# Three sets of steps in a hand-ordered FFT, MLP and mixture kernel: the middle x tile, the first S load and one load of the inverse's input

## The chip, the cores and the metric

One Trainium2 chip, one of its cores. The metric is the device time of one execution in microseconds (us), the median of several. TensorE is called PE here, VectorE DVE, ScalarE ACT, GpSimd POOL; SP is the engine whose queue issues nearly all DMAs.

## What is computed

For each of 8 batches of 3072 tokens by 256 channels: a long filter by way of the Fourier transform, then over all 24576 tokens a squared-ReLU MLP, then a soft mixture of 8 experts with 32 slots.

```python
X = np.fft.rfft(x, axis=1); y = np.fft.irfft(X * (filt_r + 1j * filt_i), n=3072, axis=1)
t = y.reshape(8 * 3072, 256)
h = np.maximum(t @ w_in, 0.0); t = h * h @ w_out
logits = t @ phi
d = softmax over tokens(logits);  slot_in = d.T @ t
slot_out[e] = np.maximum(slot_in[e] @ w1[e], 0.0) @ w2[e]
out = softmax over slots(logits) @ slot_out
```

All data is float32; the wide layer runs as three matmuls on parts of float32r, "high" and "low".

## The kernel before, in words

The tokens go through the MLP in 48 chunks of 512, six to a batch. A chunk is 8 *pairs* of the loop over `P`; a pair takes 2 steps of a common clock, so a chunk is 16 steps. In a pair, `layer` (L594, L595, L596) computes 2 x 128 features: high weights by high `xo`, high weights by low `xo`, low weights by high `xo`. `square` squares the ReLU, the odd half on POOL (L605), `turn_h` transposes it on DVE (L622), `move` sends it by DMA to a buffer `hd` in another layout (L651), and `logit` (L663) takes its product with the folded weights, in blocks of 16 matmuls every four pairs. `slot_in` (L794) multiplies `hd` of the previous chunk with the exponentials.

Between these pieces stands all other work, written into five streams (`dsp`, `mv`, `late`, `fft`, `w`) as events with a step number. `run_streams(t)` lets each stream go on in the order of its steps as far as step `t`; within one step the streams run in the order named. There is no other scheduler: the instructions stand on each engine in the order in which these functions write them, and a DMA stands on SP's queue where its function stood.

The transform of batch b runs while the batch before it goes through the MLP; its steps (`when`, `LEAD`, in the block at L1136 to L1158) count from the start of that earlier batch, so a negative step lies in the batch before that. One transform of batches 3 to 7, in its order:

- three x tiles of 1 MB (s = 0, 1, 2), each by four DMAs of 256 KB (`load_x`, L143); each is folded in two halves k = 0, 1 (`fold_x`): the sum on DVE (L155) into a small tile, the difference on POOL in place (L156). Then 16 matmuls (`mm_a`, L165), four ACT copies (L172), and two stores of 512 KB to a DRAM tensor S (`store_a`, L181).
- four blocks j: S is read back in another layout by four DMAs of 192 KB (`load_s2`, L206), 64 matmuls (`mm_b`, L299), filter products (L310, L319), 64 matmuls of the inverse (`mm_g2`, L218), copies, and four stores of 192 KB to a DRAM tensor G (`store_g2`, L240).
- for each of the batch's six chunks, `load_g` (L460) reads 512 KB of G into a tile `gin`. The matmuls `mm_y` (L514), the copy L522 and the two sums L531 on DVE make rows of y from it; `lead_y` (L539, ACT) writes the high part of `xo` in two halves, `rest_y` (L546, POOL) the low part in two halves. The first `layer` of the chunk needs all four.

The chunks with `6 * b + g` 0, 1 and 6 have a plain form instead: `mm_ai` (L478), `lead_ai`, `rest_ai`. The tiles of x, S, filter and output of the transform share three buffers of 1 MB (tag `f8`).

```python
for s, (TL, TF, T) in enumerate(TA):
    put(TL, load_x, s)
    for k in range(2):
        put(TF + k, fold_x, s, k)
...
    put(T - LS[j], load_s2, j)
```

Of the kernel before, what the change touches and what calls it, by code (L numbers as in the profile page):

```python
# [38 lines left out]
def body(tc, x, cA, cAf, fwp, fwd, ivp, inv, flt, cst, w_in, w_out, phi, w1, w2, out):  # L39
# [43 lines left out]
    def put0(t, fn, *a):  # L83
        ev0[round(t, 3)].append((fn, a))
# [369 lines left out]
    def out_events(b, st, late):  # L454
# [93 lines left out]
        for g in range(NCB):  # L548
            if 6 * b + g not in (0, 1, 6):
                T = 96 * b + 16 * g - 6.5  # L550
                late(max(T - 19.5, 13.5), load_g, g)
                late(T, mm_y, g)
                late(T + 0.5, even_y, g)
                late(T + 1, unfold, g, ALU.add)
                late(T + 1, unfold, g, ALU.subtract)
                for k in range(2):
                    late(T + 2 + 2 * k, lead_y, g, k)
                    late(T + 2.5 + 2 * k, rest_y, g, k)
                continue
            T = 96 * b + 16 * g - 4  # L560
            put = late
            if T < 0:
                def put(t, fn, *a):
                    put0(ST["G0"] + ST["Gd"] * (t + 7), fn, *a)
            put(T - (5 if (b, g) == (0, 1) else 3), load_g, g)
            if T < 0:
                put(T - 1, warm)
            for k in range(2):
                put(T + k, mm_ai, g, k)
                put(T + k + 0.5, lead_ai, g, k)  # L570
                put(T + k + 0.5, rest_ai, g, k)
# [463 lines left out]
    def stream(nm, o=0):  # L1035
        def put(t, fn, *a):
            streams[nm].append((t + o, fn, a))
        return put
# [66 lines left out]
    with tc.manual_schedule():  # L1105
        put, late = stream("fft"), stream("late")
        st = {}
        put0(43.3, load_const)
        fft_events(0, lambda: first, put0, 0, 0, 0, None, st)
        out_events(0, st, late)  # L1110
        def wput(t, *a):

# [18 lines left out]
        for n in range(4):  # L1131
# [4 lines left out]
        LEAD = [  # L1136
            [[6.5, 6.5, 9.5, 9.5], [10, 7.5, 8, 10], [5, 6, 6.5, 6.5], [5.5, 10.5, 10, 10]],
            [[5.5, 7.5, 15.25, 15.25], [6.5, 12.5, 13.5, 13.5], [5, 5.5, 10, 10], [5.5, 13, 15.25, 15.25]],
            [[20.25] + [15.25] * 3, [13.5] * 4, [20.5, 10, 10, 10], [6, 15.25, 15.25, 15.25]],
        ]  # L1140

        opened = False
# [6 lines left out]
        for b in range(1, NB):  # L1149
            st = {}  # L1150
            if b == 1:
                when = ([(22, 24.5, 26.5), (24, 29, 33.5), (27.5, 32, 36.5)], [47, 54.5, 65.5, 76.5], [53, 61.5, 70.5, 81.5])
            elif b == 2:
                when = ([(-19, -15.5, -10), (-11, -7, -3), (-5.5, -3, 0)], [13.5, 22, 38, 54], [18.5, 33.5, 49.5, 65.5])
            else:
                when = ([(-41, -31, -26), (-23, -19, -14.5), (-22.5, -15.5, -10)], [1.5, 22, 38, 54], [17.5, 33.5, 49.5, 65.5])
            fft_events(b, lambda: G["fft"], stream("fft", 96 * (b - 1)), *when, dict(f=3, u=8, c=2, lead=LEAD[min(b, 3) - 1]), st)
            out_events(b, st, late)  # L1158
        for c in range(NCH - 1):
# [241 lines left out]
        for g in range(NG):  # L1401
            b, o = divmod(g, N2 // 4)
# [171 lines left out]
```

## Time and profile before

| | |
|---|---|
| median of 3 runs | 1855.48 us (1854.55 to 1858.27) |
| the profiled execution | 1859.09 us, its span 1857.3 us |
| busy, share of the span | PE 98%, DVE 65%, ACT 56%, POOL 42% |
| granted clock of TensorE, mean | 0.996 of full speed |
| DMA queue of SP | 421 MB, 78.7% of the 16 engines' span |

The span is divided by the chunks: with two blocks of a transform in it, a chunk takes some 35.4 us, without any 31.45. PE is all but always busy, so the place to look is the few waits on PE, and who ends them. A line of the timeline is: start, duration, engine, line of the code, operation, tile written <- tiles read, shape, count, and in brackets the engine's idle time before it and who ended it. SPq is SP's queue; the duration there is the time that SP spends on issuing, with the waits inside a merged row.

### The profile page before, as it was taken

Reading aid. Unit: us, or ns where it says so; the run is one execution under the profiler, and the core shown is the slowest. Engines: PE = TensorE matmul, PEld = TensorE weight load, DVE = VectorE, ACT = ScalarE, POOL = GpSimd, SP = SyncE. Lnnn points to the kernel's source line nnn. Section 1 sums busy time; section 2 is a strip of 40 time slices with the busy share of each in tenths; the row PEclk is TensorE's granted clock in tenths of the full one; section 3 lists DMA queues with packets and bytes.
Section 4 is the critical chain, followed back from the end, with each engine's and each line's share of the span. In section 5 each row is a group of like instructions: output and inputs, shape, how many; then the busy total and the mean of one; then the engine's idle time right before and its main releaser. Section 6 shows DMA issues by size and latency. Waiting matters only on the chain.

```text
span 1857.3 us, 42036 instructions
## 1 busy us (share of the span) xinstructions
PE 1812.1 (98%) x16326; PEld 1192.9 (64%) x16326; DVE 1212.9 (65%) x2267; ACT 1033.4 (56%) x1930; POOL 776.3 (42%) x812
## 2 busy tenths in 40 slices
PE   9899999999999999999999999999999999999987
PEld 6666666666666666666666666666566666666555
DVE  7856666676666666666667666666666756565558
ACT  6755555556555564555655555556555555555445
POOL 4043543454444534544444444354344443333224
PEclk9999999999999999999999999999999999999999
DMA  8669989878777896888778787687878666675999
GB/s 309 205 184 281 257 234 269 247 212 238 230 213 203 227 273 165 224 243 214 234 220 222 209 253 220 189 229 217 247 199 240 200 169 182 171 206 153 247 338 383
DMA packets 245813, 425.02 MB, mean 229 GB/s; under 512 B 25712, under 2 KB 103664, under 8 KB 245616
## 3 DMA queue, kind: packets, MB, share of 16 engines
q1 hardware_dynamic: 244744, 421.13, 78.7%
q8 instruction: 130, 2.13, 0.5%
q10 hardware_dynamic: 728, 1.15, 0.2%
q14 instruction: 67, 0.55, 0.1%
q0 software_dynamic: 144, 0.07, 0.0%
HBM read 151.71 MB, written 77.59 MB: 123 GB/s over the span
## 4 chain that ended last, share of the span: by engine, by line
PE 84%; DMA 5%; DVE 3%; SPq 2%; issue 2%; ACT 1%; POOL 1%; POOLq 0%; DVEq 0%; ACTq 0%
PE p L594 18%; PE p L595 17%; PE p L596 17%; PE L L663 9%; PE sd L794 8%; PE sd L218 3%; PE sd L299 3%; PE sd L514 2%; PE sd L165 2%; DMA f<-S 2%; SPq L651 1%; DMA hd<-hT 1%; DVE ct L1208 1%; PE pt L1197 1%; PE pt L1410 1%
## 5 line engine op out<-in xcount | busy, mean ns | idle before, releaser
L605 POOL TENSOR_TENSOR h<-h 128x512 f32<-128x512 f32 x375 | 395.1, 1054 | 837.0 <-ACT h L601 747.5
L601 ACT ACTIVATE h<-p 128x512 f32<-128x512 f32 x768 | 459.0, 598 | 348.9 <-PE p L596 334.5
L622 DVE STREAM_TRANSPOSE hT<-h 128x512 f32<-128x512 f32 x736 | 485.3, 692 | 250.4 <-ACT h L603 230.4
L594 PE MATMUL p<-xo,wiH 128*128 128x512 f32 x1534 | 621.7, 405 | 0.1
L595 PE MATMUL p<-xo,wiH 128*128 128x512 f32 x1534 | 605.6, 395 | 7.2 <-POOL xo L546 7.2
L596 PE MATMUL p<-xo,wiL 128*128 128x512 f32 x1534 | 605.8, 395 | 0.0
L594 PEld LDWEIGHTS p<-xo,wiH 128*128 128x128 f32 x1534 | 288.1, 188 | 122.4 <-issue 43.9
L595 PEld LDWEIGHTS p<-xo,wiH 128*128 128x128 f32 x1534 | 288.6, 188 | 70.0 <-POOL xo L546 9.4
L596 PEld LDWEIGHTS p<-xo,wiL 128*128 128x128 f32 x1534 | 288.3, 188 | 68.4
L603 ACT ACTIVATE h<-h 128x512 f32<-128x512 f32 x393 | 248.4, 632 | 12.5
L319 POOL TENSOR_TENSOR u<-u 128x256 f32<-128x256 f32 x224 | 160.5, 739 | 114.9 <-DVE u L310 114.9
L663 PE MATMUL L<-h,wf 128*32 128x512 f32 x1536 | 186.9, 599 | 2.2 <-DVE wf L1021 1.8
L531 DVE TENSOR_TENSOR gin<-gin,sd 128x512 f32<-128x512 f32 x90 | 61.8, 687 | 182.7 <-ACT gin L522 181.2
L522 ACT ACTIVATE gin<-sd 128x512 f32<-128x512 f32 x45 | 26.9, 598 | 256.7 <-PE sd L514 256.7
L794 PE MATMUL sd<-hd,eT 128*32 128x512 f32 x1472 | 166.3, 592 | 0.0
L310 DVE TENSOR_TENSOR u<-sd,f 128x512 f32<-128x512 f32 x240 | 152.7, 675 | 11.5 <-PE sd L299 10.1
L546 POOL TENSOR_TENSOR xo<-gin,xo 128x512 fp32r<-128x512 f32 x90 | 119.3, 1325 | 0.0
L794 PEld LDWEIGHTS sd<-hd,eT 128*32 128x32 f32 x1472 | 47.8, 110 | 110.1 <-issue 106.8
L228 ACT ACTIVATE f<-sd 128x512 f32<-128x512 f32 x112 | 61.1, 610 | 79.8 <-PE sd L218 79.8
L713 DVE TENSOR_TENSOR lo<-L,lp 128x512 fp32r<-128x512 f32 x47 | 32.3, 688 | 107.4 <-ACT lp L712 107.4
L663 PEld LDWEIGHTS L<-h,wf 128*32 128x32 f32 x1536 | 40.0, 109 | 96.2 <-issue 91.4
L770 DVE STREAM_TRANSPOSE eT<-et 32x128 f32<-32x128 f32 x184 | 72.0, 391 | 1.9
(161 smaller groups left out, 1596.2 us busy)
## 6 DMA issues: line engine op xcount, KB each, us to landing
hd<-hT SPq DMA_DIRECT2D x736, 256.0 KB
f<-flt SPq DMA_DIRECT2D x28, 1024.0 KB
gin<-G SPq DMA_DIRECT2D x47, 512.0 KB
out<-w1t SPq DMA_DIRECT2D x47, 512.0 KB
f<-x SPq DMA_DIRECT2D x84, 256.0 KB
S<-f SPq DMA_DIRECT2D x42, 512.0 KB
f<-S SPq DMA_DIRECT2D x112, 192.0 KB
G<-f SPq DMA_DIRECT2D x112, 192.0 KB
```

The costliest lines, as they stand in the source:

```text
L310: vec.tensor_tensor(out=u, in0=p.rearrange("p (h d) -> p h d", d=D), in1=f[:, 2 * r + k:2 * r + k + 1, :].to_broadcast([128, 2, D]), op=AL ...
L319: gps.tensor_tensor(out=a[:, h, :], in0=a[:, h, :], in1=b[:, 1 - h, :], op=ALU.add if h else ALU.subtract)
L546: gps.tensor_tensor(out=lo, in0=st["gi", g][:, k::2, :], in1=hi, op=ALU.subtract)
L594: pe.matmul(p, wh, x[:, 0, kk, :], start=(kk == 0), stop=False)
L595: pe.matmul(p, wh, x[:, 1, kk, :], start=False, stop=False)
L596: pe.matmul(p, wl, x[:, 0, kk, :], start=False, stop=(kk == 1))
L601: act.activation(out=h, in_=p, func=ACTF.Relu, scale=2.0 ** -8)
L603: act.activation(out=h, in_=h, func=ACTF.Square)
L605: gps.tensor_tensor(out=h, in0=h, in1=h, op=ALU.mult)
L622: vec.transpose(hT[c, f // 8][:, f // 4 % 2, :, o:o + 128], h2[P, k].rearrange("p (b t) -> p b t", b=4))
L663: pe.matmul(lg[c][32 * n:32 * n + 32, :], wf[:, f, :], h2.pop((P + n // 2, n % 2)), start=(f < 4), stop=(f >= FT - 4), tile_position=(0, 3 ...
L794: pe.matmul(S[32 * n:32 * n + 32, :], e[:, 32 * t:32 * t + 32], v, start=(t == 0), stop=(t == 3), tile_position=(0, 32 * n),)
```

## The change

Three numbers, or sets of numbers, in the order. `when` for batches 3 to 7, tile s = 1: load at -28 instead of -23, folds from -22.5 instead of -19; its matmuls stay at -14.5. `LEAD` for the same batches, last list, first entry: the S load of block 0 stands 8 steps ahead of its matmuls instead of 6. And `load_g` in the plain form: 3 steps ahead for the one chunk whose step is negative, else 5; this alters chunk 6 (batch 1, g = 0) alone, from 3 to 5.

```diff
-            put(T - (5 if (b, g) == (0, 1) else 3), load_g, g)
+            put(T - (3 if T < 0 else 5), load_g, g)
...
-            [[20.25] + [15.25] * 3, [13.5] * 4, [20.5, 10, 10, 10], [6, 15.25, 15.25, 15.25]],
+            [[20.25] + [15.25] * 3, [13.5] * 4, [20.5, 10, 10, 10], [8, 15.25, 15.25, 15.25]],
...
-                when = ([(-41, -31, -26), (-23, -19, -14.5), (-22.5, -15.5, -10)], [1.5, 22, 38, 54], [17.5, 33.5, 49.5, 65.5])
+                when = ([(-41, -31, -26), (-28, -22.5, -14.5), (-22.5, -15.5, -10)], [1.5, 22, 38, 54], [17.5, 33.5, 49.5, 65.5])
```

The order of PE and that of ACT are the same before and after, buffer numbers aside. On the other engines three places differ. The first is SP's queue around the load of the middle x tile of batch 3 (`f_5468` before, `f_5370` after; `f_5033` is the tile s = 0, `f_5479` or `f_5482` the tile s = 2, `f_5330` the last output tile of batch 2). Before:

```order
L881 DMA c_dr<-co 128x128
L240 DMA G<-f_5330 48x4x256 x4
L460 DMA gin<-G 128x1024
L181 DMA S<-f_5033 128x1024 x2
L143 DMA f_5468<-x 64x2x512 x4
L143 DMA f_5479<-x 64x2x512 x4
L651 DMA hd<-hT 128x1x512 x8
```

And now:

```order
L881 DMA c_dr<-co 128x128
L143 DMA f_5370<-x 64x2x512 x4
L240 DMA G<-f_5330 48x4x256 x4
L460 DMA gin<-G 128x1024
L181 DMA S<-f_5033 128x1024 x2
L143 DMA f_5482<-x 64x2x512 x4
L651 DMA hd<-hT 128x1x512 x8
```

The four x loads passed the four stores to G, the load of `gin` and two stores to S.

The second place is SP's queue a chunk later, where S of the same batch is complete and its first block is read (`f_5954` before, `f_5855` after). Before:

```order
L181 DMA S<-f_5468 128x1024 x2
L460 DMA gin<-G 128x1024
L181 DMA S<-f_5479 128x1024 x2
L651 DMA hd<-hT 128x1x512 x8
L206 DMA f_5954<-S 48x4x256 x4
L651 DMA hd<-hT 128x1x512 x8
```

And now:

```order
L181 DMA S<-f_5370 128x1024 x2
L460 DMA gin<-G 128x1024
L181 DMA S<-f_5482 128x1024 x2
L206 DMA f_5855<-S 48x4x256 x4
L651 DMA hd<-hT 128x1x512 x16
```

The S loads passed eight moves of h. (In batch 1 the one load of `gin` passed the two S stores of a tile in the same way, so that two loads of `gin` stand together.)

The third is POOL around the two low parts of `xo` of the first chunk after the fold, with the folds of the middle x tile. Before:

```order
L605 TENSOR_TENSOR h<-h 128x512 x5
L546 TENSOR_TENSOR xo<-gin,xo 128x512
L156 TENSOR_TENSOR f_5468<-f_5468 128x512
L605 TENSOR_TENSOR h<-h 128x512
L546 TENSOR_TENSOR xo<-gin,xo 128x512
L156 TENSOR_TENSOR f_5468<-f_5468 128x512
L605 TENSOR_TENSOR h<-h 128x512
L156 TENSOR_TENSOR f_5479<-f_5479 128x512 x2
```

And now:

```order
L605 TENSOR_TENSOR h<-h 128x512 x3
L156 TENSOR_TENSOR f_5370<-f_5370 128x512
L605 TENSOR_TENSOR h<-h 128x512
L156 TENSOR_TENSOR f_5370<-f_5370 128x512
L605 TENSOR_TENSOR h<-h 128x512
L546 TENSOR_TENSOR xo<-gin,xo 128x512
L605 TENSOR_TENSOR h<-h 128x512
L546 TENSOR_TENSOR xo<-gin,xo 128x512
L605 TENSOR_TENSOR h<-h 128x512
L156 TENSOR_TENSOR f_5482<-f_5482 128x512 x2
```

Both folds of the tile passed the first `xo` write. On DVE the two sums L155 of this tile moved with them: the first from behind L781 to the place ahead of the last transpose before L531, the second to the place right behind the two L531, ahead of L855.

## Rows read from the trace of the kernel before

**Rows 1.** Waits of PE, 427 to 1391 us: total us, times, longest.

```profile
PE p L595 <- POOL xo L546: 7.2, 5, 1.4
PE sd L299 <- DMA f<-S: 4.1, 9, 1.0
```

**Rows 2.** Timeline of PE where chunk 17 begins.

```profile
676.46 0.40 PE L596 MATMUL p<-xo,wiL 128*128 128x512 f32 x1
676.70 0.40 PE L594 MATMUL p<-xo,wiH 128*128 128x512 f32 x1
678.54 0.50 PE L595 MATMUL p<-xo,wiH 128*128 128x512 f32 x1 [1.44 <-POOL xo L546]
```

**Rows 3.** Timeline of POOL around the start of chunk 17.

```profile
671.54 1.04 POOL L605 TENSOR_TENSOR h<-h 128x512 f32<-128x512 f32 x1 [8.60 <-ACT h L601]
...
674.52 1.30 POOL L156 TENSOR_TENSOR f<-f 128x512 f32<-128x512 f32 x1 [0.63 <-DMA hd<-hT]
675.77 1.49 POOL L605 TENSOR_TENSOR h<-h 128x512 f32<-128x512 f32 x1
677.23 1.26 POOL L546 TENSOR_TENSOR xo<-gin,xo 128x512 fp32r<-128x512 f32 x1
```

**Rows 4.** Timeline of POOL and PE at the start of chunk 18, without folds.

```profile
711.44 1.04 POOL L605 TENSOR_TENSOR h<-h 128x512 f32<-128x512 f32 x1 [0.45 <-ACT h L601]
712.44 1.29 POOL L546 TENSOR_TENSOR xo<-gin,xo 128x512 fp32r<-128x512 f32 x1
...
714.03 0.40 PE L595 MATMUL p<-xo,wiH 128*128 128x512 f32 x1
```

**Rows 5.** Windows from L663 to the L594 behind L299: length, busy, clock, DMA, GB/s.

```profile
210.40:214.14 3.74, 3.74 (x82) 1.59 (x81) 1.59 (x3) 1.19 (x2) 1.04 (x1) 1.00 1.00 342
502.48:507.56 5.08, 4.36 (x81) 1.84 (x81) 3.26 (x6) 1.20 (x2) 1.63 (x2) 1.00 1.04 278
715.99:721.85 5.86, 5.08 (x82) 1.83 (x81) 2.93 (x5) 1.19 (x2) 1.29 (x2) 1.00 1.07 260
930.32:935.32 5.00, 4.42 (x81) 1.60 (x80) 3.27 (x6) 1.19 (x2) 1.63 (x2) 1.00 1.08 244
1143.75:1149.77 6.02, 4.59 (x82) 1.71 (x81) 2.71 (x5) 1.20 (x2) 1.08 (x2) 1.00 1.03 267
1358.21:1363.73 5.52, 4.91 (x81) 1.82 (x81) 2.80 (x5) 1.19 (x2) 1.17 (x2) 1.00 1.03 279
```

**Rows 6.** Timeline of SP's queue, 693 to 715 us, and PE's first wait.

```profile
693.57 1.30 SPq L181 DMA_DIRECT2D S<-f  x2
703.64 8.42 SPq L651 DMA_DIRECT2D hd<-hT  x8
712.11 2.89 SPq L206 DMA_DIRECT2D f<-S  x4
...
718.14 0.59 PE L299 MATMUL sd<-f,fw 48*32 48x256 f32 x2 [0.22 <-DMA f<-S]
```

**Rows 7.** Timeline of DVE, 668 to 675 us.

```profile
668.29 1.41 DVE L531 TENSOR_TENSOR gin<-gin,sd 128x512 f32<-128x512 f32 x2 [5.52 <-ACT gin L522]
...
672.65 1.78 DVE L155 TENSOR_TENSOR u<-f 128x512 f32<-128x512 f32 x1
```

**Rows 8.** Timeline of SP and PE at the load for chunk 6.

```profile
266.93 0.59 SPq L460 DMA_DIRECT2D gin<-G  x1
...
276.10 0.35 PE L478 MATMUL sd<-cst_t,gin 128*128 128x128 f32 x1 [0.81 <-DMA gin<-G]
```

**Rows 9.** Timeline of SP and PE, 649 to 668 us.

```profile
649.93 3.32 SPq L240 DMA_DIRECT2D G<-f  x4
656.06 0.34 SPq L460 DMA_DIRECT2D gin<-G  x1
...
657.81 6.47 SPq L143 DMA_DIRECT2D f<-x  x8
...
666.41 1.16 PE L514 MATMUL sd<-cst_t,gin 64*64 64x64 f32 x64
```

## The prediction

> **What bounds the kernel now.** I read first which waits end on TensorE, then the places of those waits in the timelines, then the queue of SP around the moved DMAs. From 427 to 1391 us, the stretch in which batches 3 to 7 are transformed, PE waits for two things alone: five times for `xo`, written by POOL, and nine times for S tiles that a DMA brings [rows 1]. All else on PE runs there without a gap. So PE sets the end, and only what removes or adds a PE wait changes the time; the other engines matter where PE waits for them.
>
> The `xo` wait: matmuls of the layer start 0.24 us after one another, but the L595 at 678.54 starts 1.84 us after its forerunner [rows 2]. It reads the low part of `xo`, which POOL wrote from 677.23 to 678.49. Ahead of that write on POOL stand the first fold of the middle x tile (L156, 1.30 us, itself waiting 0.63) and a square of 1.49 [rows 3]. Where no fold is in between, the same write begins at 712.44 and PE takes its product at 714.03 without a wait [rows 4].
>
> The S wait: at the first block of a transform a logit, L663, is followed by the 64 matmuls L299 and then by L594. From the start of L663 to that L594 it is 3.74 us where S is there, and 5.08, 5.86, 5.00, 6.02 and 5.52 us in the five batches concerned [rows 5]. The waits of [rows 1] add to less, since the profile counts gaps between modelled ends and each break also costs a refill; I take the distances. SP shows why S is late: the S stores go out at 693.57, SP then stands until the moves of h begin at 703.64, eight of these take 8.42 us, and the first S load is issued at 712.11 [rows 6].
>
> **The change part by part.**
>
> *Fold of the middle x tile earlier (load from step -23 to -28, fold from -19 to -22.5), five batches.* No instruction is added: four x loads, two DVE adds and two POOL subtracts per batch move. On POOL both folds now stand before the first `xo` write, and between the two `xo` writes there is only the square, as in the undisturbed chunk. Gain per batch: 1.84 - 0.24 = 1.60 us, times five is 8.0 us. What could take it back is the new place of the second fold. Its DVE add follows the two L531, which end at 668.29 + 1.41 = 669.70 [rows 7]. Those two adds of the same shape last 0.7 each; the old place of the fold shows 1.78, beside a running POOL operation [rows 7]. The subtract (1.30) then ends between 671.7 and 672.8. The square that used to start at 671.54, after 8.60 us of idleness [rows 3], is late by 0.2 to 1.2 us, and the `xo` writes behind it by as much. In the undisturbed chunk POOL idles 0.45 before the square between the two `xo` writes, and the second of them ends 0.30 before PE's start [rows 4]; so some 0.7 us of lateness costs nothing. I take the lower value, as POOL is idle when this add runs: no residue. The upper bound leaves 0.5 us per batch, 2.5 in all. The first fold lies further ahead: its add delays one transpose by 0.7 to 1.8 us before DVE idles 5.52 us for L531 [rows 7], and its subtract delays one square inside POOL's 8.60 [rows 3]. Nothing waits for these two sooner.
>
> *S load earlier (lead 6 to 8), five batches.* The four loads now stand ahead of sixteen moves of h. They must wait for the last S store (issued by 694.9). In the present place the first S load is issued at 712.11 and PE's wait for it ends at 718.14, 6.0 us later in a crowded queue [rows 6]. So S would be asked for at about 700 and be there by 708, ten us before it is used. Even if SP could issue these loads only when the moves now begin, at 703.64, the four would be out by 706.5 (four took 2.89) [rows 6] and there by 712.5. Gain: (5.08 + 5.86 + 5.00 + 6.02 + 5.52) - 5 x 3.74 = 8.8 us. Below that I see no bound but the rival below; above it there is nothing left to win, since 3.74 is the work itself. The moves pass from before the S loads to behind them, at worst 2.9 us later; the matmuls that read them come a whole chunk later, 35 us.
>
> *One load of the inverse's input (batch 1) two steps earlier.* It passes two S stores of 512 KB. PE idles 0.81 us for it before the L478 at 276.10 [rows 8]. Two such stores hold SP for 1.30 us elsewhere [rows 6], so the load goes out earlier by more than PE waits, and its bytes come earlier still: 0.8 us gained, with nothing at the lower end should the queue in front of it be the limit. The two S stores land later by one load; their reader is a later chunk.
>
> *The queues passed.* On SP the x loads now go ahead of four G stores, one `gin` load (which waits for these stores) and two S stores, and behind these stay the other x tile and the moves. That is the only new wait in the change; it is priced as a rival.
>
> **Sum.** 8.0 + 8.8 + 0.8 = 17.6 us. The profiled execution took 1859.1 us (span 1857.3) and would take 1841.5; the median of the runs is 1855.48, 3.6 lower, and becomes **1837.9 us**. (Only more than 0.2%, some 3.7 us, can be told from no change.)
>
> **The rivals.**
>
> *The `xo` wait stays in part.* The second fold's add is slowed and the squares take 1.49 instead of 1.04, as one of them does in [rows 3]: late by up to 1.2 + 0.45, less 0.7 of slack, about 1 us per batch. That gives 1838.5 to 1843. For it speaks that the write has so little slack; against it, that POOL stands still while DVE adds, since it waits for that very add.
>
> *The S load is no earlier* (the change would not do what it says): each DMA on SP may wait for others, and the first S load must wait for the S stores. It would have to be held some 12 us, until 712, to leave the wait as it is: 1837.9 + 8.8 = 1846.7. Nothing in [rows 6] holds SP between 695 and 703.
>
> *The G stores come late, and the kernel is slower.* Today the stores go out from 649.93, the last has landed when `gin` is issued at 656.06, and the matmuls L514 on it start at 666.41 [rows 9]. With four x loads ahead the stores shift by 3.2 us if only the issues count (eight took 6.47), by 4.3 us if the 1.05 MB of x must be moved first, at the 244 GB/s of the slowest stretch with all DMA engines busy [rows 5]. So `gin` goes out at 659.3 to 660.4. No row shows how long this one takes. From below: the last G store, 192 KB, landed 2.8 us after its issue ended [rows 9]. From above: the load issued at 266.93, with two stores just ahead of it, was waited for until 276.10, 9.2 us [rows 8]. So `gin` lands between 662.1 and 669.6; I take about 5 us, nearer to the first since the queue is empty at that point, hence 664.3 to 665.4, before 666.41. Each us after 666.41 costs 5 us in five batches. At the upper end, 3.2 us late, 16 us are lost and 1853.9 is left. The kernel turns slower by over 0.2% from 4.3 us late, a landing after 670.7; at 5 us late it takes 1862.9. The page "DMA: Bandwidth & Descriptors" of the Trainium skill (Queues, rings and completion order) has each DMA engine consume descriptors in the order of its ring: by it the shift is the one by bytes, not by issues. The sum stays the same by both, but the margin shrinks from 2.1 to 1.0 us, and by it this rival has 5 in 100 instead of 2; no row shows yet which holds, and I keep the 5, as the x bytes have to move in either case.
>
> **How the numbers follow.** All three waits gone, 1837.9: 0.78. `xo` in part: 0.10. S still late: 0.05. G late: 0.05, of it 0.02 with a loss too small to eat the gain, 0.01 about even, 0.02 slower. Something else: 0.02, halved between same and slower. So faster 0.95, same 0.02, slower 0.03. The forecast's own spread is that of the runs, 1854.55 to 1858.27, less 17.6: 1837.0 to 1840.7. Below I add some 2 us for the refill after each broken stream of layer matmuls, which I left out of the first term; above, the `xo` rival up to 1843. Range **1834.8 to 1843.0**.
>
> **What would show it.** Right: in the profile after, PE's waits for `xo` L546 and for f<-S are gone between 427 us and the end of the last transform; POOL's second `xo` write starts 1.6 us before the L595 that reads it in the five chunks too; from L663 to L594 it is 3.74 in all five; L478 has no idle time before it. Wrong: PE waits at L514 for `gin`, or at L595 still for `xo`, or SP issues the S loads only after the moves began.

## The result, and the profile after

| | before | changed kernel |
|---|---|---|
| median of the runs | 1855.48 us (1853.55 to 1858.27, 5 runs) | 1842.27 us (1838.5 to 1845.28, 5 runs) |
| ratio | | 0.9916, 95% interval 0.9901 to 0.9932 |
| profiled execution, its span | 1859.09, 1857.3 us | 1842.09, 1840.3 us |
| chunks 11 to 36 (of the span) | 927.96 us | 910.95 us |
| chunks 5 and 6 | 39.80 + 35.62 us | 38.74 + 36.45 us |
| from the start of chunk 47 to PE's last matmul | 131.01 us | 132.25 us |

The changed kernel is faster by 13.2 us in the medians and by 17.0 in the two profiles. The forecast was 1837.9 in a range of 1834.8 to 1843.0, so the time lies within, near the upper end. (Chunk lengths are distances on PE's timeline from the first L594 of one chunk to that of the next.)

What was seen in [rows 1] is gone: between 427 and 1391 us PE now waits for nothing. The longest of its waits in the whole span are these, all in the start and in the end (line, for whom: total us, times, longest).

```profile
PE pt L1197 <- DVE ct L1208: 5.9, 21, 0.6
PE pt L1319 <- DVE lt L760: 2.1, 1, 2.1
PE L L663 <- DVE wf L1021: 1.8, 1, 1.8
PE pt L1365 <- DMA wx<-w: 1.6, 1, 1.6
```

The stretch as a window shows the same: PE is busy for the whole of it, where before it was busy for 916.63 of 927.96 us (length, then busy time of PE, PEld, DVE, ACT, POOL, and the clock).

```profile
460.65:1371.60 910.95, 910.95 (x8214) 596.21 (x8212) 589.63 (x1124) 513.83 (x954) 413.15 (x423) 1.00 0.81 226
```

To [rows 2 and 3] answers POOL's timeline of the changed kernel where chunk 17 begins, at 671.18:

```profile
665.58 1.30 POOL L156 TENSOR_TENSOR f<-f 128x512 f32<-128x512 f32 x1 [5.26 <-DVE u L155]
666.83 1.04 POOL L605 TENSOR_TENSOR h<-h 128x512 f32<-128x512 f32 x1
667.83 1.30 POOL L546 TENSOR_TENSOR xo<-gin,xo 128x512 fp32r<-128x512 f32 x1
669.53 1.04 POOL L605 TENSOR_TENSOR h<-h 128x512 f32<-128x512 f32 x1 [0.40 <-ACT h L601]
670.53 1.29 POOL L546 TENSOR_TENSOR xo<-gin,xo 128x512 fp32r<-128x512 f32 x1
```

The fold L156 stands ahead of the first `xo` write, and between the two writes there is one square, at its 1.04 and not the 1.49 of before. The second write ends at 671.82; PE's L595 on it starts at 672.12 without a wait, the same 0.30 us as in the undisturbed chunk of [rows 4]. The DVE add of this fold follows the two L531 at once, and takes 0.68, not the 1.78 of [rows 7]:

```profile
663.49 1.41 DVE L531 TENSOR_TENSOR gin<-gin,sd 128x512 f32<-128x512 f32 x2 [4.92 <-ACT gin L522]
664.81 0.68 DVE L155 TENSOR_TENSOR u<-f 128x512 f32<-128x512 f32 x1
```

The windows from L663 to the L594 behind L299, to be held against [rows 5], have all come down to the 3.74 us of the undisturbed one; PE is busy in each for as long as the window is:

```profile
498.96:502.70 3.74, 3.74 (x81) 1.59 (x80) 2.00 (x4) 1.20 (x2) 1.04 (x1) 1.00 0.81 208
709.50:713.24 3.74, 3.74 (x81) 1.59 (x80) 2.00 (x4) 1.20 (x2) 1.04 (x1) 1.00 0.79 213
920.06:923.80 3.74, 3.74 (x82) 1.59 (x81) 2.00 (x4) 1.20 (x2) 1.04 (x1) 1.00 0.67 142
1130.61:1134.35 3.74, 3.74 (x81) 1.59 (x81) 2.01 (x4) 1.20 (x2) 1.04 (x1) 1.00 0.72 162
1341.16:1344.90 3.74, 3.74 (x81) 1.59 (x80) 2.00 (x4) 1.20 (x2) 1.04 (x1) 1.00 0.82 191
```

SP's queue and PE at that place (to [rows 6]): the S loads go out at 693.70, all sixteen moves behind them, and L299 starts 17.7 us later.

```profile
693.70 2.24 SPq L206 DMA_DIRECT2D f<-S  x4
697.15 17.13 SPq L651 DMA_DIRECT2D hd<-hT  x16
...
711.36 1.96 PE L299 MATMUL sd<-f,fw 48*32 48x256 f32 x64
```

At chunk 6 (to [rows 8]) L478 has lost its wait, but something else has come. Here are SP, PE, DVE and POOL around it, each from its own timeline:

```profile
263.96 0.93 SPq L460 DMA_DIRECT2D gin<-G  x2
...
270.04 3.08 SPq L651 DMA_DIRECT2D hd<-hT  x4
273.16 4.24 SPq L143 DMA_DIRECT2D f<-x  x4
```

```profile
273.50 1.05 PE L478 MATMUL sd<-cst_t,gin 128*128 128x128 f32 x8
...
282.67 0.69 DVE L155 TENSOR_TENSOR u<-f 128x512 f32<-128x512 f32 x1 [0.88 <-DMA f<-x]
...
283.44 1.27 POOL L156 TENSOR_TENSOR f<-f 128x512 f32<-128x512 f32 x1 [1.08 <-DVE u L155]
...
284.77 1.08 PE L165 MATMUL sd<-f,ca_t 64*64 64x512 f32 x4
285.77 0.50 PE L594 MATMUL p<-xo,wiH 128*128 128x512 f32 x1
```

The last x tile of batch 2 is loaded behind four moves of h, as it was before, and as long after the start of chunk 5 (29.7 us, before 29.8); PE now comes to its L165 1.1 us sooner. DVE stands for the tile before it can fold, POOL stands for DVE, and the L165 on that fold now breaks: the 16 matmuls from 283.03 take 2.74 us up to L594, where before they took 1.91:

```profile
285.71 0.65 PE L165 MATMUL sd<-u,ca_t 64*64 64x512 f32 x2
...
287.62 0.50 PE L594 MATMUL p<-xo,wiH 128*128 128x512 f32 x1
```

Chunk 5 gained 1.06 us and chunk 6 lost 0.83.

### The profile page after: what moved, and what is told of

The parts are those of the page before. It is cut to its first block, busy times and chain, and to the rows that moved or that the text cites. A ratio compares the mean times of both kernels' runs of the same rounds, so it can differ in the third digit from the quotient of the medians.

```text
span 1840.3 us, 42101 instructions
## 1 busy us (share of the span) xinstructions
PE 1807.3 (98%) x16326; PEld 1192.8 (65%) x16326; DVE 1204.0 (65%) x2267; ACT 1033.9 (56%) x1930; POOL 774.7 (42%) x812
## 4 chain that ended last, share of the span: by engine, by line
PE 92%; DMA 3%; DVE 1%; issue 1%; ACT 1%; SPq 0%; DVEq 0%; ACTq 0%
PE p L594 20%; PE p L596 19%; PE p L595 19%; PE L L663 9%; PE sd L794 9%; PE sd L299 3%; PE sd L218 3%; PE sd L514 3%; PE sd L165 2%; DMA wx<-w 1%; DMA wx<-wo_dr 1%; DVE ct L1208 1%; PE pt L1197 1%; PE sd L265 1%; PE pt L1410 1%
## 5 line engine op out<-in xcount | busy, mean ns | idle before, releaser
L594 PE MATMUL p<-xo,wiH 128*128 128x512 f32 x1534 | 622.6, 406 | 0.1
L595 PE MATMUL p<-xo,wiH 128*128 128x512 f32 x1534 | 605.8, 395 | 0.0
L594 PEld LDWEIGHTS p<-xo,wiH 128*128 128x128 f32 x1534 | 288.3, 188 | 122.9 <-issue 44.3
L595 PEld LDWEIGHTS p<-xo,wiH 128*128 128x128 f32 x1534 | 289.0, 188 | 61.2
L663 PE MATMUL L<-h,wf 128*32 128x512 f32 x1536 | 186.9, 599 | 2.2 <-DVE wf L1021 1.8
L531 DVE TENSOR_TENSOR gin<-gin,sd 128x512 f32<-128x512 f32 x90 | 61.8, 687 | 179.7 <-ACT gin L522 178.1
L546 POOL TENSOR_TENSOR xo<-gin,xo 128x512 fp32r<-128x512 f32 x90 | 119.4, 1326 | 0.0
L663 PEld LDWEIGHTS L<-h,wf 128*32 128x32 f32 x1536 | 40.0, 109 | 96.2 <-issue 91.3
L156 POOL TENSOR_TENSOR f<-f 128x512 f32<-128x512 f32 x42 | 54.0, 1285 | 68.9 <-DVE u L155 58.6
```

The lines of the kernel that those rows point to most:

```text
L546: gps.tensor_tensor(out=lo, in0=st["gi", g][:, k::2, :], in1=hi, op=ALU.subtract)
L594: pe.matmul(p, wh, x[:, 0, kk, :], start=(kk == 0), stop=False)
L595: pe.matmul(p, wh, x[:, 1, kk, :], start=False, stop=False)
L663: pe.matmul(lg[c][32 * n:32 * n + 32, :], wf[:, f, :], h2.pop((P + n // 2, n % 2)), start=(f < 4), stop=(f >= FT - 4), tile_position=(0, 3 ...
```

## The experiments

In the first four, the kernel before had a median of 1857.43 us (1855.03 to 1863.62, 14 runs) on the same chip; in the next four 1857.03 (1855.77 to 1860.71, 8 runs); in the last two 1858.24 (1853.64 to 1862.01, 7 runs).

**The whole change again.** No edit.

> The changed kernel once more. Theory F (the median's 13 against the profile's 17 us is the scatter of start and end): chunks 11 to 36 again take 17.0 us less than before in the profile, the five distances are 3.74; before chunk 11 and after chunk 47 begins the span differs by 1 to 3 us from the other profile; the ratio's interval takes in 0.9908. Rival G (some executions keep a stall): one of the ten waits is back in this profile.

Measured: 1843.07 us (1841.09 to 1843.36, 4 runs), ratio 0.9912, interval 0.9895 to 0.9928. Chunks 11 to 36 took 910.73 us in its profile, chunks 5 and 6 38.74 + 36.42, the end 134.06. PE's gain in the middle repeats to 0.2 us, and so does what chunk 6 gives back: F holds, G falls.

**The x tile alone.**

```diff
-(-41, -31, -26), (-23, -19, -14.5), (-22.5, -15.5, -10)
+(-41, -31, -26), (-28, -22.5, -14.5), (-22.5, -15.5, -10)
```

> The x tile's load and fold alone. Theory A (the two stalls are separate, and S follows PE, since the moves ahead of the S loads wait for slot_in on PE): no wait for xo at L595; L663 to the L594 behind L299 still 5.0 to 6.0 us in the five batches; 8.5 us less in all. Rival B (S lands at a time of its own, set by the DMAs): PE comes 1.7 us earlier to the same landing, the five distances grow to 6.7 to 7.7, and nearly nothing is gained.

Measured: 1850.74 us (1846.83 to 1856.35, 10 runs), ratio 0.9961, interval 0.9946 to 0.9975. Of the two waits of [rows 1] one is left (the profile's list of PE's waits, same stretch):

```profile
PE sd L299 <- DMA f<-S: 3.2, 7, 0.9
```

The five chunks after the fold take 35.42 us each, as in the changed kernel, against 37.10 before. From L663 to the L594 behind L299 it is 5.49, 7.09, 4.84, 5.58 and 5.75 us; in the batch of 7.09 the granted clock fell (last section), the other four lie about where [rows 5] has them. So the x steps remove the `xo` wait and nothing else: A holds, and B, by which S would have come in its own time and all five distances would have grown to 6.7 us and more, falls.

**The S load alone.**

```diff
-[6, 15.25, 15.25, 15.25]
+[8, 15.25, 15.25, 15.25]
```

> The S load alone. Theory A: the five distances from L663 to L594 are all 3.74 us, the xo wait at L595 stays at 1.44 five times, 8.8 us less in all; with the first run 17.3, the sum of the two. Rival C (the S load needs the earlier x load, whose stores then come earlier): the S loads are held on SP until about 712, and nothing is gained.

Measured: 1850.7 us (1848.53 to 1854.7, 5 runs), ratio 0.9959, interval 0.9945 to 0.9973. All five distances are 3.74 us, and the other wait stays to the tenth:

```profile
PE p L595 <- POOL xo L546: 7.2, 5, 1.4
```

C falls. The two parts add up, within their intervals: 0.39% and 0.41% against 0.88% for the whole.

**The load of gin alone.**

```diff
-put(T - (5 if (b, g) == (0, 1) else 3), load_g, g)
+put(T - (3 if T < 0 else 5), load_g, g)
```

> The one load of the inverse's input alone. Theory D (the wait is only handed on): L478 no longer waits, 1.0 us earlier, but the L165 of chunk 6 then wait some 0.9 us for the fold of batch 2's last x tile, which a DMA sets; by 290 us next to nothing is gained. Rival E (the later wait at L165 comes from the other two parts or from the run): 1.0 us is gained and L165 runs as in the kernel before.

Measured, one execution: 1861.0 us, among those of the kernel before. Chunk 5 is at 38.74 us without a wait at L478, chunk 6 at 36.93; the sum, 75.67, stands beside 75.42 in the profile of before. D holds: what PE gains ahead of L478 it gives back at L165:

```profile
287.07 1.08 PE L165 MATMUL sd<-f,ca_t 64*64 64x512 f32 x4 [0.19 <-POOL f L156]
```

**Which half of the x move does it: the load alone.**

```diff
-(-23, -19, -14.5)
+(-28, -19, -14.5)
```

> The kernel before with one number changed: the load of the middle x tile of batches 3 to 7 at step -28, its folds staying at -19. Theory A (the order on POOL makes the wait: a fold stands between the two writes of xo): PE's wait for xo by L546 stays at five times some 1.4 us, 7.2 in all, and the time is that of before within 2 us. Rival B (the late data makes the wait: before, the fold itself stood 0.63 us for its x tile): with x there five steps sooner the wait falls by 0.6 a batch or more, to 4 us in all or less.

Measured, one execution: 1856.27 us. PE's waits in the stretch begin with `PE p L595 <- POOL xo L546: 7.2, 5, 1.5`. POOL's timeline shows the row order of [rows 3] with the same numbers, though x lay there five steps earlier; even the fold's 0.63 us of idleness is unchanged, so that was never a wait for x. It fits the DVE add L155 of the same half, which lasts 1.79 us from 670.99 and ends 0.08 us before the fold starts; the fold overwrites what this add reads.

```profile
672.86 1.30 POOL L156 TENSOR_TENSOR f<-f 128x512 f32<-128x512 f32 x1 [0.63 <-DMA hd<-hT]
674.11 1.49 POOL L605 TENSOR_TENSOR h<-h 128x512 f32<-128x512 f32 x1
675.56 1.26 POOL L546 TENSOR_TENSOR xo<-gin,xo 128x512 fp32r<-128x512 f32 x1
```

Theory A holds: the order on POOL makes the wait.

**The fold alone.**

```diff
-(-23, -19, -14.5)
+(-23, -22.5, -14.5)
```

> The kernel before with one number changed: the folds of the middle x tile of batches 3 to 7 at step -22.5, the load staying at -23. Theory A (only the place of the folds matters; the x tile, issued from 657.81 in the kernel before, is there by some 667.6, inside DVE's idle time ahead of the two L531 at 668.29): the wait for xo is gone or under 1 us in all, and the time falls by 6 to 9 us, the whole x term. Rival B (the load has to move too): DVE stands at the first L155 for the x tile past 668.29, L531 and all of xo come late by as much, and PE waits for xo more than the 1.4 us of before in each of five batches, so the time does not fall and may rise by up to 10 us.

Measured: 1849.94 us (1846.87 to 1853.69, 5 runs), ratio 0.9958, interval 0.9942 to 0.9974: as much as load and fold together. The `xo` wait is gone. DVE does wait for x, but inside the time in which it had nothing to do:

```profile
662.37 0.69 DVE L155 TENSOR_TENSOR u<-f 128x512 f32<-128x512 f32 x1 [3.11 <-DMA f<-x]
...
665.38 1.41 DVE L531 TENSOR_TENSOR gin<-gin,sd 128x512 f32<-128x512 f32 x2 [1.70 <-ACT gin L522]
666.71 0.68 DVE L155 TENSOR_TENSOR u<-f 128x512 f32<-128x512 f32 x1
```

L531 starts when ACT's copy ends, as before; of the idle time ahead of it 1.70 us is left. So the earlier load buys nothing that PE can see. Rival B falls.

**The slower rival, with the load doubled.** Behind the first four loads of the tile stand the same four again, into the same tile (`load_x` is altered to allow that; the lines are left out here):

```diff
+            if b > 2 and s == 1:
+                put(TL, load_x, s, True)
```

> The changed kernel, with the middle x tile of batches 3 to 7 loaded a second time, by the same four DMAs right behind the first four, so that eight instead of four stand ahead of the G stores, and the second four wait for the first. It prices the rival of the prediction that ends slower. Theory A (gin has 1.6 to 2.6 us to spare in the changed kernel; four more loads, with their wait, put it off by 5 to 6 us): PE waits for gin at L514 five times, some 3 us each, 15 us in all, and the time rises to some 1857, which is that of the kernel before. Rival B (the slack is larger than it seems, or the second four go beside the stores): no wait at L514, and the time of the changed kernel within 2 us.

Measured: 1842.6 us (1841.21 to 1843.45, 4 runs), ratio 0.9919, interval 0.9902 to 0.9935. Theory A is wrong, and with it the price of the rival in the prediction. SP's queue and PE there (the edit moves the lines: L463 is the load of gin, L517 is `mm_y`):

```profile
644.80 8.12 SPq L144 DMA_DIRECT2D f<-x  x8
652.97 2.71 SPq L241 DMA_DIRECT2D G<-f  x4
658.70 0.34 SPq L463 DMA_DIRECT2D gin<-G  x1
...
661.68 1.16 PE L517 MATMUL sd<-cst_t,gin 64*64 64x64 f32 x64
```

The load goes out 12.57 us ahead of chunk 17 (which starts at 671.27), in the changed kernel 16.55, so it is 4.0 us later. Yet PE runs through L517, 3 us after the issue, without a wait, in all five batches. It could, because L517 at 661.68 does not read that load. The code says so:

```python
late(max(T - 19.5, 13.5), load_g, g)
late(T, mm_y, g)
```

A chunk's `gin` is loaded 19.5 steps ahead of its own `mm_y`, and a chunk is 16 steps. The load beside the x loads is for the next chunk's product, which starts at 697.10; even if it took the 9.2 us of [rows 8] to land, it would have 29 us to spare, not one or two.

**Mending what chunk 6 gives back.** The changed kernel, with the last x tile of batch 2 loaded ahead of the four moves:

```diff
-(-19, -15.5, -10), (-11, -7, -3), (-5.5, -3, 0)
+(-19, -15.5, -10), (-11, -7, -3), (-6.5, -3, 0)
```

> The changed kernel with one more number changed: the load of the last x tile of batch 2 at step -6.5 instead of -5.5, ahead of four moves of h. Theory A (the 0.8 us that chunk 6 gained ahead of L478 are lost again in the same chunk because the fold of that tile waits for its load, and PE's L165 for the fold): DVE no longer waits for x at L155 there, PE's break at L165 is gone, chunk 6 takes some 35.6 us instead of 36.45, and the profile is 0.8 us shorter; in the medians no more than 0.8, at the edge of what they can tell. Rival B (the folds wait for something else, or the moves that come later make a new wait): chunk 6 stays at 36.2 us or more.

Measured: 1841.16 us (1839.09 to 1844.44, 4 runs), ratio 0.9911, interval 0.9895 to 0.9927. On DVE the wait ahead of the second add is gone (282.67 in the changed kernel), of the first 0.71 of 2.85 us is left:

```profile
278.82 0.69 DVE L155 TENSOR_TENSOR u<-f 128x512 f32<-128x512 f32 x1 [0.71 <-DMA f<-x]
...
281.43 0.69 DVE L155 TENSOR_TENSOR u<-f 128x512 f32<-128x512 f32 x1
```

Chunk 6 takes 35.58 us and chunk 5 stays at 38.74: theory A for the place, and 0.87 us off the stretch. (In the other profiles with the new load of `gin` and this x load in its old place, chunk 6 takes 36.42 to 37.34, and 39.12 in the run with lead 3.) Whether the kernel is faster than the changed one by that much can't be told: the intervals of the two all but coincide, and this profile's span, 1842.7, is longer by its start and end.

**How the S wait depends on the queue: lead 3.** The changed kernel with twelve moves ahead of the S loads (before: eight, changed: none).

```diff
-[8, 15.25, 15.25, 15.25]
+[3, 15.25, 15.25, 15.25]
```

> The changed kernel with the S load of block 0 of batches 3 to 7 at lead 3 instead of 8: twelve moves of h stand ahead of the four loads on SP's queue, where the kernel before has eight and the changed kernel none. Theory A (each move ahead puts the S loads off by its own 1.05 us, and PE stands for all of it): four moves more than before, 4.2 us, on the excess of before (8.8 us in five batches, 1.76 each) make 6.0 us a batch and 30 us in all; the distance from L663 to L594 is some 9.7 us in each of the five, and the time some 1872. Rival B (the wait is made by the landing of S, not by the moves ahead): the distances stay at before's 5 to 6 us, time some 1851. Rival C on the clock (three of the five profiles so far with this wait show the granted clock at 0.5 to 0.6 for some us at 716 to 728, none of the five without it): a longer break brings the clock down more often, seen in two or more of the five batches, at 3 us and more each on top of A; else the clock stays at 1.00 there but for one place.

Measured: 1881.04 us (1880.36 to 1884.07, 4 runs), ratio 1.0125, interval 1.0102 to 1.0147. The five distances are 10.27, 10.17, 9.63, 10.57 and 10.51 us, 32.4 in all above 3.74, near A's 30. SP and PE in chunk 18, and PE's list of waits:

```profile
707.47 12.25 SPq L651 DMA_DIRECT2D hd<-hT  x12
719.76 3.13 SPq L206 DMA_DIRECT2D f<-S  x4
...
725.17 0.59 PE L299 MATMUL sd<-f,fw 48*32 48x256 f32 x2 [3.42 <-DMA f<-S]
...
PE sd L299 <- DMA f<-S: 19.7, 11, 3.8
```

Twelve moves take 12.25 us, 1.02 each, and the S loads stand behind them. PE's waits for S are 19.7 us in all, before 4.1 [rows 1]: four more moves, 4.1 us of SP's time, add 3.1 us of waiting a batch. So A holds in kind, but that its sum comes so near is in part luck: from the first L299 to L594 it takes 4.60 to 5.11 us in these batches, 1.88 in the changed kernel, and part of that is matmuls at a lower clock. The rest of the lost time is rival C: the chunks are longer by 41.1 us in sum, 8.7 more than the distances. The windows of chunk 18 (the two numbers to read are PE's busy time, first behind the length, and the clock, third from the end) show why:

```profile
719.82:725.17 5.35, 1.93 (x18) 0.45 (x18) 1.30 (x2) 1.20 (x2) 1.04 (x1) 1.00 0.96 238
725.17:730.00 4.83, 4.29 (x65) 1.57 (x65) 2.77 (x5) 0.00 (x0) 1.40 (x2) 0.70 1.00 288
730.00:733.40 3.40, 3.40 (x14) 2.72 (x9) 0.32 (x1) 0.44 (x1) 1.45 (x3) 0.50 0.90 259
733.40:736.00 2.60, 2.60 (x11) 2.06 (x11) 1.75 (x3) 1.39 (x3) 0.38 (x1) 0.89 1.01 195
```

**Lead 7.** Four moves ahead of the S loads.

```diff
-[8, 15.25, 15.25, 15.25]
+[7, 15.25, 15.25, 15.25]
```

> The changed kernel with the S load of block 0 of batches 3 to 7 at lead 7 instead of 8: four moves of h stand ahead of the loads instead of none. Theory A (1.05 us a move): the loads go out 4.2 us sooner than before, more than the 1.3 to 2.3 us that each batch lost, so no wait of L299 for S, five distances of 3.74 us, and the time of the changed kernel within 2 us, with a margin of some 2 us for S. Rival B (the loads need the room ahead of all moves): a wait for S stays, up to 1 us a batch, and the time is 2 to 5 us above the changed kernel's.

Measured: 1842.99 us (1841.68 to 1845.81, 4 runs), ratio 0.9923, interval 0.9903 to 0.9943; all five distances 3.74 us, no wait of L299 for S, 910.72 us for chunks 11 to 36. With four moves ahead S is in time:

```profile
697.57 3.30 SPq L651 DMA_DIRECT2D hd<-hT  x4
700.98 3.53 SPq L206 DMA_DIRECT2D f<-S  x4
```

Rival B falls: one step of lead would have done, since four moves (3.3 us) are more than each batch lost.

## Why the prediction was right, and where it was not

**The xo term, 8.0 us: right in mechanism and size.** The term read PE's start on the late product against its place in the stream, 1.60 us a batch; on the changed kernel L595 comes 0.94 us into the chunk and not 2.55, and the chunk is shorter by 1.68. The 0.08 more, five times, goes with the break in the stream: the matmul behind the late L595 starts 0.34 us after it, others 0.24. The prediction left this out of the term and put some 2 us for it into the range; it is 0.4 in all. The residue was rightly taken as none: the second add took 0.68, the squares 1.04. The rival that `xo` stays in part fell with it. One part of the reasoning was idle: the load of x did not have to move (the fold alone gives the whole gain).

**The S term, 8.8 us: right.** The distances fell by exactly what [rows 5] had above 3.74, and the order on SP was the cause: with 0 and 4 moves of h ahead no wait, with 8 the wait of before, with 12 a larger one. Between 8 and 12 moves PE's waiting grew by 3.1 us a batch, while the four moves take 4.1 us on SP. (What the distances say beyond that holds a share of the lower clock.) The rival that S is no earlier fell: nothing held SP between 695 and 703 us.

**The term for gin at chunk 6, 0.8 us: wrong.** The prediction named no work that would be late next. It is the last x tile of batch 2, whose fold PE reaches in chunk 6: chunk 5 and 6 together gained 0.23 us, not 0.81. Even the 0.23 is less than the scatter: the two take 75.4 to 76.4 us in five profiles with this load in its old place, 75.2 to 76.1 in five with the new (77.9 with lead 3), so no gain of this term can be told from the runs. The wait itself also comes and goes. The fold alone leaves this load where it was and shows 39.68 + 36.58 us; the x load alone, which leaves it too, shows 38.74 + 37.52: no wait at L478, and the time is lost at L165. So the end of chunk 6 is set by x, and what is saved at L478 is spent at L165; with that x load earlier the two chunks take 74.32 us.

**The rival that ended slower: wrong in its place.** It took L514 at 666.41 for the reader of the gin load beside it [rows 9]. The two rows are near each other on the clock, but the steps in the code put the reader a chunk later, and with the load 4.0 us later still PE did not wait. The shift itself came near the forecast: the load goes out 16.55 us ahead of chunk 17's start, before 19.93 us ahead of where that chunk began (675.99), so 3.4 us later. The row lies between the 3.2 by issues and the 4.3 by bytes. By the rule of the page "DMA: Bandwidth & Descriptors" of the Trainium skill (Queues, rings and completion order), that descriptors are consumed in ring order, it should have been the second. The trace doesn't settle it, as the load also waits for the stores to land.

**The sum, 17.6 us.** Between chunk 11 and the end of chunk 36 the changed kernel took 17.0 us less, against 16.8 for the two terms. The medians moved by less, 13.2 us, and by 14.4 when both kernels were run again. Part of that is the execution that was profiled: at 1859.09 it was slower than all five timed runs of before, and chunk 5 began at 245.12 in it, at 242.3 to 245.7 in the others. Part is the median that the sum was taken from: 1855.48 is of few runs, and the 29 runs of the same kernel in the experiments have medians of 1857.03 to 1858.24. Another part lies in the end, where chunk 47 and what follows took 131.0, 130.4 and 131.7 us in the three profiles of kernels with both waits in place, and 132.3, 134.1, 134.0, 131.7 and 131.7 in the five with both gone. PE's wait at L1365 for expert weights is 0 to 0.3 us in the first and 1.0 to 3.4 in the second; yet the two do not go together run by run, for the end takes 131.7 us without that wait (the load alone) and with 2.6 us of it (the load doubled, L1368 there). Why that load, which no edit moves, is later there is left open; no run was aimed at it. So of the 4.4 us between forecast and result some 0.6 is the gin term, and the failed step behind the rest is the last one: a sum read off one execution was taken from the median unchanged, as if start and end would stay. How that rest divides is not shown.

## What to carry to other kernels

Cost a wait by PE's own timeline, and look for its cure in the order, at what stands on the queue or engine just ahead of the late item. That is not the price: eight moves took 8.42 us of SP and cost PE 1.76 us a batch, since the rest was slack, and moving the loads past four of them was enough. Before a waiting load is asked for earlier, look for what the next stage waits for, since a gain can be given back one chunk on. And match a DMA to its reader by the tile and the steps that the code gives both, never by nearness on the timeline.

## What was not expected of the hardware

A wait of PE can cost more than its own length, when the granted clock falls with it. With lead 3 the granted clock fell in each of the five chunks, in which PE stood 2.6 to 3.8 us for S ahead of the first L299 (in chunk 18 it was busy for 1.93 of 5.35 us there): to 0.50, the 1.2 GHz level, and in chunk 18 back to 1.00 by some 735 us. In the kernels with the smaller S wait it happened in some executions only: one of five batches in three of the five profiles, each time in chunk 18, at about 716 to 728 us, and nowhere between 427 and 1391 us in the six profiles without this wait. What decides it is not shown: the kernel before has its longest distance, 6.02 us, at a clock of 1.00 [rows 5]. The fold alone is one of these three, chunk 18 (the clock is third from the end):

```profile
711.40:715.70 4.30, 3.07 (x42) 1.07 (x48) 1.30 (x2) 1.19 (x2) 1.04 (x1) 1.00 1.03 227
715.70:718.74 3.04, 2.90 (x54) 0.93 (x38) 2.45 (x5) 0.00 (x0) 1.08 (x2) 0.66 1.02 338
718.74:723.30 4.56, 4.56 (x17) 3.59 (x12) 0.94 (x3) 1.23 (x2) 1.75 (x3) 0.50 0.86 244
723.30:728.00 4.70, 4.70 (x22) 3.79 (x21) 4.67 (x9) 2.59 (x5) 2.69 (x4) 0.98 1.04 258
```

That chunk took 39.09 us, 33.33 undisturbed and 35.46 in the kernel before, where the S wait was there and the clock stayed up. The page "TensorE: Matmul & The Clock Gate" of the Trainium skill (HAM oscillation — how this bites in real kernels) describes this: a wait for a DMA between two pieces of compute lets the clock fall, so the next piece starts at the lower level. The trace agrees that the clock fell in all five batches of lead 3, but only in one of them had it fallen when L299 began; in the other four the granted clock was 1.00 for the first 1.0 to 2.5 us of L299. So the S term of 8.8 us is a lower figure for an execution in which the clock stays up; the removed wait also removes the chance of such a fall.
